# Attention and gated block on one core: the third block's end in halves, projections ahead of a part's rest, units in the last block, rows and weights fetched ahead

## The chip, the core and the metric

The kernel runs on one core of a Trainium2 chip. Its engines work side by side, each on its own list of instructions in order, and wait for one another through semaphores: TensorE (PE) multiplies matrices, VectorE (DVE) and ScalarE (ACT) work element by element, GpSimd (POOL) takes a few element-wise steps, SyncE (SP) issues transfers. The metric is the device time of one execution in microseconds; lower is better.

## The reference

The input x has 2048 rows of 640 bf16 values. A is attention with 32 heads of 20 columns, B a gated product of two projections of width 1728.

```python
h  = x + A(layernorm(x), wqkv, wo)
h2 = h + B(layernorm(h), w_gate, w_up, w_down)
# A: q, k, v = x @ wqkv; p = softmax(q @ k.T * 20 ** -0.5); o = p @ v; o @ wo
# B: g = x @ w_gate; u = x @ w_up; (g * u) @ w_down
```

## The kernel before

The 2048 queries are four blocks of 512 (`NB`, `QB`). The heads are eight groups of four (`NG`, `HPG`), each head in a slot of 32 partitions, so that four heads' score matmuls run in four row strips of the array. A segment is one group's scores of one block against all keys. `PASS` says which query columns a segment's name stands for: "0" to "3" are whole blocks, "A" and "B" the two halves of the last block. The order of `segs` is the order of the attention work: blocks 0, 1 and 2 over all groups, then block 3 whole for two groups (`SPLIT_G`), then its half A for the other six, then its half B. The score columns are cut into 683 tiles of 1536 (three PSUM banks), two tiles in flight. The main loop runs over the tiles: `emit_S` issues the score matmuls (L490) and the exponential of the tile on ACT (L503), `emit_AV` the products with the values (L677) of a tile two or three back, and `run_job` fits other PE work between them, in pieces.

A tile can give its last bank of 512 columns to DVE: `emit_x` computes these exponentials in four DVE operations (L528, L537, L538, L533). Such a piece is called a unit here. `x_takes` (L514) decides by the planner's times (`at`) whether DVE is free; in the last block it takes a unit only where no job is queued or running.

The planner works out the whole order in Python while the program is built: `at` holds its estimate of when PE, DVE and ACT are done, `jobs` is the queue of PE work, `urgent` goes ahead of it, `waiting` holds jobs that stand aside until their input should be ready, `aux` holds DVE work done in spare time, `later` runs a step some tiles on. `keep_warm` (L460) issues two matmuls that nobody reads where PE would idle (recorded at L463).

A finished segment is normalised. Most go through `norm`: the sums of the exponentials travel to DRAM and back (SP: sums, r16, scr, four of bc), DVE takes reciprocals, and POOL multiplies into `On` (L600). The last one of a part (`FAST`) is done by `job_norm` on PE (L608, L624, L639). A block's multiply waits until the projection of the block before has read `On` (the key "om").

When a part is normalised, `add_tail` queues its rest: rows of x and weights are loaded ("load"), `job_out` projects with wo and adds x (L914, L918), takes the layer norm in `aux` and transposes (L271), `job_glu` makes gate times up (`glu_sum`, groups of 512 columns, L980; `glu_pair`, both products of 256 columns in one bank, L998), `job_y` multiplies with w_down (L1035, L1039) and stores. All of these share one PSUM bank, `mi`. The parts are blocks 0, 1 and 2 and the last block's first half (row tiles 0 and 1). Its second half is done after the last exponential by `last_tail`; while its layer norm runs on DVE and ACT, `fill` lets PE finish the jobs that are left over. At the first tile of the last block `load_res` fetches the weights of the column groups 3 to 6 into the buffers of q, which are free by then.

Of the kernel before, what the change touches and what calls it, by code (L numbers as in the profile page):

```python
# [56 lines left out]
EXP_NS, EXP_END, EXP_COL = 50, 166, 5 / 6  # L57
S_NS, S_EXP, SWITCH, LAT = 323, 500, 110, 150
TOL, LEAST, MARGIN = 200, 430, 100
WO_NS, SUMS_NS, ROOT_NS, ROWS_NS = 1500, 6000, 5000, 5000  # L60
END_OF_TIME = 10 ** 9
X_LEAST, X_OUT, X_SOON = 3, 6, 4
# [15 lines left out]
def kernel(  # L78
# [233 lines left out]

    PASS = {"0": (0, 0, QB), "1": (1, 0, QB), "2": (2, 0, QB), "3": (3, 0, QB), "A": (3, 0, HW), "B": (3, HW, HW)}
    segs = []
    for ch in range(NB):
        for g in range(G1):
            kind = "copy" if ch == 0 else "last" if ch == NB - 1 else "add"
            segs.append(("0", g, ch * TPB, (ch + 1) * TPB, kind))  # L320
    segs += [("0", g, 0, NT, "only") for g in range(G1, NG)]
    segs += [(p, g, 0, NT, "only") for p in "12" for g in range(NG)]
    segs += [("3", g, 0, NT, "only") for g in range(SPLIT_G)]
    segs += [(p, g, 0, NT, "only") for p in "AB" for g in range(SPLIT_G, NG)]
    FINAL = len(segs) - 1
    FAST = {("2", NG - 1), ("A", NG - 1), ("B", NG - 2)}

    tiles, cur_t, pos = [], [], 0
    for s, (p, g, lo, hi, _) in enumerate(segs):
# [56 lines left out]
    def step():  # L386
        if cur["fresh"] and (first() or waiting):
            if cur["gen"] is not None:
                jobs.appendleft((cur["key"], cur["gen"]))
            cur["key"], cur["gen"] = (urgent if first() else waiting).popleft()  # L390
        c = advance()
        if c == WAIT:
            waiting.append((cur["key"], cur["gen"]))
            cur["gen"] = None
            c = advance() if jobs and jobs[0][0][0] == "y" else NEXT
        if c is None:
            return None
# [67 lines left out]
    def run_job(until):  # L465
        if cur["fresh"]:
            key = urgent[0][0] if first() else cur["key"] if cur["gen"] is not None else jobs[0][0] if jobs else None
            begin = max(at["pe"], at["mi"], opens.get(key, 0))
            if not waiting and key not in free_keys and (key is None or begin + SWITCH + COST.get(key[0], LEAST) > until):
                return key is not None  # L470
        begun = at["pe"]
        while at["pe"] + 216 <= until + 60:
            c = step()
            if c == FREE and cur["key"][0] not in ("spill", "load"):
                return run_job(until)
            if c in (None, NEXT, END, FREE):
                break
        return at["pe"] > begun

    def emit_S(i):  # L480
# [29 lines left out]
        for s, kt, j, o in us:  # L510
            if o < n_act:
                av_q.append((i, s, kt, j, e[:, o:o + PASS[segs[s][0]][2]]))

    def x_takes(i):  # L514
        us, n = tiles[i]
        s = us[-1][0]
        return (n == EW and segs[s][4] == "only" and (PASS[segs[s][0]][0] < LAST_B or not jobs and not cur["gen"]) and last_tile[s] - i >= X_LEAST and len({u[0] for u in us}) == 1
                and len(x_open) < 2 and at["dve"] < at["pe"] + TOL and len(x_live) < X_OUT)

    def emit_x(ps, us):  # L520
# [46 lines left out]
    def need_x(s):  # L567
        while x_left.get(s):
            step_x()

    def norm(s, asb):
        p, g = segs[s][0:2]
        b, c0, w = PASS[p]
# [9 lines left out]
        def back():  # L583
            if at["pe"] < due and now["i"] < n_tiles:
                later(1, back)
                return
            ri = nrm.tile([P, n], F32, name="ri", tag=f"ri{n}")
            dve(240)
            nc.vector.reciprocal(ri[:], r16)
            scr = dram.tile([HPG, w], F32, name="scr", tag=f"scr{w}")  # L590
            nc.sync.dma_start(scr[:].rearrange("j (c f) -> (j c) f", f=n), ri[:])
            bc = nrm.tile([P, QB], F32, name="bc")
            for j in range(HPG):
                nc.sync.dma_start(bc[SLOT * j:SLOT * (j + 1), 0:w], scr[j:j + 1, :].to_broadcast([SLOT, w]))

            def mult():
                if b and ("om", b - 1) not in done:
                    later(1, mult)
                    return
                nc.gpsimd.tensor_tensor(On[g][:, c0:c0 + w], asb[:, 0:w], bc[:, 0:w], ALU.mult)  # L600
                done.add(("n", p, g))
            later(8, mult)
# [24 lines left out]
    def job_norm(s, asb):  # L627
# [7 lines left out]
        ps = rows_to_cols(bc, w, bank())  # L635
        yield 1030 * w // QB
        dve(690 * w // QB)
        assert b == 0 or ("om", b - 1) in done
# [239 lines left out]
    def open_late():  # L878
        rx.release()
        ra.release()  # L880
        late["wd"] = pool("lwd", side="right")
        late["w"] = pool("lw", 2, side="right")
        late["h"] = pool("lh", side="right")
        late["s"] = pool("ls", 2, side="right")
        late["Wd"] = [late["wd"].tile([P, D], BF16, name=f"wd{f}") for f in range(2 * FP)]

    def load_wd():
# [2 lines left out]
            nc.sync.dma_start(late["Wd"][f][0:rows, :], B_w_down[f * P:f * P + rows, :])  # L890

    def new_st(rows_of):
        hp = late["h"]
        st = {"rows": rows_of, "xr": {}}
        st["ln2T"] = hp.tile([P, KT, QB], BF16, name="ln2T")
# [40 lines left out]
    def job_out(on, st, ts, key):  # L936
# [32 lines left out]

    def load_res():  # L970
        for k, fp in enumerate(range(RES0, FP)):
            late["res"][fp] = [w_tile(src, fp, qkp.tile([P, QA], BF16, name=f"qa{2 * k + m}", tag=f"qa{2 * k + m}"))
                               for m, src in enumerate((B_w_up, B_w_gate))]

    def glu_sum(st, fp, f2, k, c0, n, hold):
        w = min(FPW, FF - fp * FPW)
# [29 lines left out]
                yield 216 * n // QB  # L1006
        yield NEXT

    def job_glu(st, ts, order=tuple(range(FP))):
        c0, n = ts[0] * P, len(ts) * P  # L1010
        hold = {}
        if "hh" not in st:
# [39 lines left out]

    LAST_B, LAST_T = NB - 1, [2, 3]

    def add_tail(b, ts):
        if b == 0:
            do(("open",), open_late)
        key = (b, ts[0])

        def ready():  # L1060
            if b not in tail_st:
                tail_st[b] = new_st(rows_of(b))
                tail_st[b]["res"] = late["res"]
            load_tail(tail_st[b], ts)
            load_w(0, tail_st[b])
            if b == 0:
                load_w(1, tail_st[b])
                load_wd()

        def lazy(fn):  # L1070
            yield from fn(tail_st[b])
        early = b == LAST_B and ("y", b - 1, 0) in done and ("y", b - 1, 1) not in done
        if early:
            free_keys.add(("load",) + key)
            urgent.append((("load",) + key, once(ready)))
        else:
            do(("load",) + key, ready)
        if b == 0:
            add(("pause",), slots(3))
        out = ("out",) + key, lazy(lambda st: job_out(On, st, ts, key))  # L1080
        if early:
            urgent.append(out)
        else:
            jobs.append(out)
        add(("glu",) + key, lazy(lambda st: job_glu(st, ts)))
        if b == LAST_B:
            do(("loadB",), load_last)
        if b == LAST_B:
            y = lazy(lambda st: job_y(st, ts))
            add(("y",) + key, some(y, 2 * len(ts) - 1))  # L1090
            held.append((("y", b, "end"), y))
        else:
            for k in range(2):
                add(("y", b, k), lazy(lambda st, k=k: job_y(st, ts[2 * k:2 * k + 2])))
        if b == 0:
            for g in range(NG):
                do(("spill", g), lambda g=g: spill(g))
# [106 lines left out]
    b_seen, a_seen = 0, False  # L1204
    i = 0
    while i < n_tiles or av_q:
        now["i"] = i
# [17 lines left out]
        if b_seen < NB - 1 and normed(str(b_seen), range(NG)):  # L1225
            add_tail(b_seen, list(range(TPB)))
            b_seen += 1
        if not a_seen and normed("3", range(SPLIT_G)) and normed("A", range(SPLIT_G, NG)):
            add_tail(LAST_B, [0, 1])
            a_seen = True  # L1230
# [111 lines left out]
```

## Time and profile before

| | us |
|---|---|
| median of 3 runs | 939.32 (938.56 to 939.32) |
| the profiled execution, its own time | 938.44 |
| its span, first to last instruction | 936.4 |
| first exponential starts | 15.66 |
| last exponential ends | 894.12 |
| from there to the end of the span | 42.3 |
| ACT busy | 887.8 |
| PE busy | 818.6 |
| DVE busy | 620.7 |

The page gives busy times of the engines and, in 40 slices of the span, their busy shares in tenths. A line of a group names the source line, the engine, the operation, what it writes and reads, the shapes and the count; behind the first bar stand busy time and mean duration in ns, behind the second the idle time just before and who ended it. PE busy is not PE at its peak, since matmuls overlap.

### The profile page before, as it was taken

Reading aid. Unit: us, or ns where it says so; the run is one execution under the profiler, and the core shown is the slowest. Engines: PE = TensorE matmul, PEld = TensorE weight load, DVE = VectorE, ACT = ScalarE, POOL = GpSimd, SP = SyncE. Lnnn points to the kernel's source line nnn. Section 1 sums busy time; section 2 is a strip of 40 time slices with the busy share of each in tenths; the row PEclk is TensorE's granted clock in tenths of the full one; section 3 lists DMA queues with packets and bytes.
Section 4 is the critical chain, followed back from the end, with each engine's and each line's share of the span. In section 5 each row is a group of like instructions: output and inputs, shape, how many; then the busy total and the mean of one; then the engine's idle time right before and its main releaser. Section 6 shows DMA issues by size and latency. Waiting matters only on the chain.

```text
span 936.4 us, 18059 instructions
## 1 busy us (share of the span) xinstructions
PE 818.6 (87%) x7138; PEld 321.7 (34%) x7219; DVE 620.7 (66%) x1222; ACT 887.8 (95%) x719; POOL 61.6 (7%) x155
## 2 busy tenths in 40 slices
PE   8788888888987898998898898998888889978897
PEld 5233232222232222332233222332332334435565
DVE  7674359898888888887888888887562331133342
ACT  6999999999999999999999999999999999999941
POOL 3310011000000000000000000000000000000000
PEclk9999999999999999999999999999899999999999
DMA  6000010011150022014120312002402000212310
GB/s 190 29 2 1 1 27 25 13 35 27 41 164 7 27 77 63 13 34 169 56 57 2 91 48 62 20 29 62 120 2 70 15 12 20 64 28 56 78 43 18
DMA packets 67818, 44.44 MB, mean 47 GB/s; under 512 B 18504, under 2 KB 63404, under 8 KB 67728
## 3 DMA queue, kind: packets, MB, share of 16 engines
q1 hardware_dynamic: 67728, 43.23, 16.6%
q8 instruction: 58, 0.95, 0.4%
q14 instruction: 32, 0.26, 0.1%
HBM read 35.91 MB, written 7.30 MB: 46 GB/s over the span
## 4 chain that ended last, share of the span: by engine, by line
ACT 51%; PE 24%; issue 18%; DVE 7%; ACTq 0%
ACT E L503 51%; PE sc L490 5%; PE acc L677 4%; PE mi L980 3%; PE mi L1035 3%; PE mi L291 2%; PE f L980 2%; PE f L1035 1%; PE mi L305 1%; PE mi L463 1%; DVE xt L538 1%; DVE st L193 1%; DVE u L258 1%; DVE kT L298 1%; PE mi L998 1%
## 5 line engine op out<-in xcount | busy, mean ns | idle before, releaser
L503 ACT ACTIVATE E<-sc 128x1536 bf16<-128x1536 f32 (+1 forms) x683 | 870.3, 1459 | 8.8 <-PE sc L490 6.4
L490 PE MATMUL sc<-qa,kT 32*128 32x512 bf16 x1536 | 201.1, 384 | 47.5 <-ACT E L503 37.0
L490 PEld LDWEIGHTS <-kT 32*128 32x128 bf16 x2432 | 83.8, 91 | 282.8 <-issue 236.1
L677 PE MATMUL acc<-E,vx 128*32 128x512 bf16 (+1 forms) x2305 | 168.2, 351 | 0.5 <-ACT E L503 0.5
L528 DVE TENSOR_SCALAR xv<-sc 128x512 f32<-128x512 f32 x127 | 86.9, 688 | 32.3 <-PE sc L490 31.6
L538 DVE SCALAR_TENSOR_TENSOR xt<-xt,xv 128x512 f32<-128x512 f32 x127 | 92.6, 737 | 0.7
L533 DVE SCALAR_TENSOR_TENSOR xe<-xt,xv 128x512 int16<-128x512 f32 x127 | 90.8, 720 | 0.8
L291 PE MATMUL mi<-lnT,wp 128*128 128x512 bf16 x280 | 81.8, 381 | 10.4 <-DVE kT L298 3.8
L537 DVE SCALAR_TENSOR_TENSOR xt<-xv 128x512 f32<-128x512 uint16 x127 | 87.5, 704 | 0.3
L490 PE MATMUL sc<-qb,kT 32*128 32x256 bf16 (+1 forms) x896 | 69.1, 291 | 16.5 <-ACT E L503 13.3
L600 POOL TENSOR_TENSOR on<-asb,bc 128x512 bf16<-128x512 f32 (+1 forms) x30 | 36.5, 1216 | 694.6 <-DMA bc<-scr 547.7
L677 PEld LDWEIGHTS <-vx 128*32 128x32 bf16 x2432 | 44.4, 95 | 64.3 <-issue 63.8
L1035 PE MATMUL mi<-wd,hh 128*128 128x320 bf16 x364 | 64.3, 302 | 2.0 <-DVE xr L1039 2.0
L258 DVE CAST u<-mi 128x512 bf16<-128x512 f32 (+1 forms) x42 | 29.0, 690 | 36.1 <-PE mi L980 31.7
L1035 PEld LDWEIGHTS <-hh 128*128 128x128 bf16 x448 | 38.4, 97 | 39.9 <-issue 28.3
L980 PE MATMUL mi<-ln2T,wg 128*128 128x512 bf16 (+1 forms) x161 | 45.8, 382 | 6.9 <-DVE u L258 6.4
L463 PE MATMUL mi<-kT,ident 128*128 128x512 bf16 x151 | 48.6, 390 | 1.8 <-issue 0.5
L980 PE MATMUL mi<-ln2T,wu 128*128 128x512 bf16 (+1 forms) x157 | 45.2, 387 | 5.7 <-DVE hh L988 4.7
L988 DVE TENSOR_TENSOR hh<-mi,u 128x512 bf16<-128x512 f32 (+1 forms) x42 | 28.8, 685 | 25.4 <-PE mi L980 22.9
L291 PEld LDWEIGHTS <-wp 128*128 128x128 bf16 x310 | 25.0, 97 | 52.9 <-issue 39.1
L914 PE MATMUL mi<-wo,on 128*128 128x320 bf16 x224 | 38.6, 301 | 2.4 <-DVE xr L918 2.3
L298 DVE TENSOR_SCALAR kT<-mi,one_row 128x512 bf16<-128x512 f32 x30 | 22.4, 746 | 26.7 <-PE mi L291 26.5
(151 smaller groups left out, 582.6 us busy)
## 6 DMA issues: line engine op xcount, KB each, us to landing
bc<-scr SPq DMA_DIRECT2D x100, 64.0 KB
wu<-in_B_w_up_dram SPq DMA_DIRECT2D x20, 320.0 KB
wg<-in_B_w_gate_dram SPq DMA_DIRECT2D x20, 320.0 KB
qsp<-qa SPq DMA_DIRECT2D x8, 384.0 KB
xr<-in_A_x_dram SPq DMA_DIRECT2D x16, 160.0 KB
out_dram<-xr SPq DMA_DIRECT2D x14, 160.0 KB
wd<-in_B_w_down_dram SPq DMA_DIRECT2D x13, 160.0 KB
xs<-in_A_x_dram SPq DMA_DIRECT2D x3, 640.0 KB
```

Of the source, the lines that this page charges most:

```text
L291: nc.tensor.matmul(ps[:], lhsT=wslice(m, g, c), rhs=lnT[:, c, ch * QB:(ch + 1) * QB], start=(c == 0), stop=(c == KT - 1))
L463: nc.tensor.matmul(ps[:], lhsT=ident[:], rhs=kT[0][:, 0:BANK], start=True, stop=True)
L490: nc.tensor.matmul(sc[:, o:o + w], lhsT=kT[g][SLOT * j:SLOT * (j + 1), kt * P:(kt + 1) * P], rhs=q_of(g, b, c0, w)[SLOT * j:SLOT * (j + 1) ...
L503: exps = nc.scalar.activation(e[:, 0:n_act], sc[:, 0:n_act], ACT.Exp, bias=EXP_BIAS, scale=SM_SCALE)
L528: took = nc.vector.tensor_scalar(v[:], ps, X_SCALE, X_BASE, ALU.mult, ALU.max)
L533: nc.vector.scalar_tensor_tensor(e[:], t[:], X_R, v[:], ALU.mult, ALU.add)
L537: lambda: nc.vector.scalar_tensor_tensor(t[:], u, X_P, u, ALU.add, ALU.mult),
L538: lambda: nc.vector.scalar_tensor_tensor(t[:], t[:], X_Q, u, ALU.add, ALU.mult),
L677: nc.tensor.matmul(acc["t"][SLOT * j:SLOT * (j + 1), 0:w], lhsT=vx[kt][:, VS * h:VS * h + SLOT], rhs=e, start=(acc["n"][j] == 0), stop=(ac ...
L914: nc.tensor.matmul(ps[:, 0:HALF], lhsT=on[g][:, t * P:(t + 1) * P], rhs=wo[g][:, cs], start=(g == 0), stop=(g == NG - 1))
L980: nc.tensor.matmul(ps[0:M, 0:n], lhsT=st["w", fp][k][:, c, f2 * P:f2 * P + M], rhs=st["ln2T"][:, c, c0:c0 + n], start=(c == 0), stop=(c == ...
L1035: nc.tensor.matmul(ps[:, 0:HALF], lhsT=st["hh"][f][0:K, t * P:(t + 1) * P], rhs=late["Wd"][f][0:K, cs], start=(f == 0), stop=(f == 2 * FP ...
```

## The change

The third block is now split as the last one was: two groups whole, then two halves "C" and "D" for the other six. Its rest is queued in two parts of two row tiles. A part's projection goes on the urgent queue if its rows are there already (`rows_early` loads them when the part whose buffers they take is queued to its last product), so that it runs ahead of what is left of the part before. A job that stands aside now lets any other part's job go on, where before only the "y" jobs could. Units may be taken in the whole groups and the first half of the last block, and in its second half while a job stands aside. The first weights of the next part are fetched at the last column group of the part before, and the resident weights of the last block one every three tiles instead of all at once. `ln2T` is one buffer for all parts instead of one a part.

```diff
+RES_STEPS = 3
...
-    PASS = {"0": (0, 0, QB), ... "A": (3, 0, HW), "B": (3, HW, HW)}
+    PASS = {"0": (0, 0, QB), ... "C": (2, 0, HW), "D": (2, HW, HW), "A": (3, 0, HW), "B": (3, HW, HW)}
...
-    segs += [(p, g, 0, NT, "only") for p in "12" for g in range(NG)]
-    segs += [("3", g, 0, NT, "only") for g in range(SPLIT_G)]
-    segs += [(p, g, 0, NT, "only") for p in "AB" for g in range(SPLIT_G, NG)]
+    segs += [("1", g, 0, NT, "only") for g in range(NG)]
+    for full, halves in ("2", "CD"), ("3", "AB"):
+        segs += [(full, g, 0, NT, "only") for g in range(SPLIT_G)]
+        segs += [(p, g, 0, NT, "only") for p in halves for g in range(SPLIT_G, NG)]
-    FAST = {("2", NG - 1), ("A", NG - 1), ("B", NG - 2)}
+    TAILS = {0: [0], 1: [0], 2: [0, 2]}
+    FAST = {("C", NG - 1), ("D", NG - 1), ("A", NG - 1), ("B", NG - 2)}
...
-            c = advance() if jobs and jobs[0][0][0] == "y" else NEXT
+            c = advance() if jobs and not any(w[0][1:] == jobs[0][0][1:] for w in waiting) else NEXT
...
-            if not waiting and key not in free_keys and (key is None or begin + SWITCH + COST.get(key[0], LEAST) > until):
+            if waiting:
+                if begin + SWITCH + COST["T"] > until:
+                    return True
+            elif key not in free_keys and (key is None or begin + SWITCH + COST.get(key[0], LEAST) > until):
                 return key is not None
...
+    def X_LAST(p):
+        return p != "B" or bool(waiting)
...
-  ... (PASS[segs[s][0]][0] < LAST_B or not jobs and not cur["gen"]) ...
+  ... (PASS[segs[s][0]][0] < LAST_B or X_LAST(segs[s][0])) ...
...
+    def read_out(b):
+        return all(("om", b, t) in done for t in TAILS[b])
...
-                if b and ("om", b - 1) not in done:
+                if b and not read_out(b - 1):
...
+        late["ln2T"] = late["h"].tile([P, KT, QB], BF16, name="ln2T")
...
-            x_t = late["s"].tile([P, D], BF16, name="xr", bufs=TPB)
+            x_t = late["s"].tile([P, D], BF16, name="xr", bufs=TPB + 2)
...
-                done.add(("om", key[0]))
+                done.add(("om",) + key)
...
     def load_w(fp, st):
-        if fp in st["res"]:
+        if fp == 0 and "next" in late:
+            st["w", fp] = late.pop("next")
+        elif fp in st["res"]:
...
     def load_res():
         for k, fp in enumerate(range(RES0, FP)):
...
+                later(RES_STEPS * (2 * k + m), one)
...
+            if more and k == FP - 1:
+                ahead = {"res": {}}
+                load_w(0, ahead)
+                late["next"] = ahead["w", 0]
...
+    rows_in = set()
+    HELD_BY = {(1, 0): [(0, 0)], (2, 0): [(0, 2)], (2, 2): [(1, 0)], (3, 0): [(1, 2)]}
...
+    def rows_early(b, ts):
+        key = b, ts[0]
+        if key in HELD_BY and key not in rows_in and all(("y",) + k in done for k in HELD_BY[key]):
+            rows(b, ts)
...
-        early = b == LAST_B and ("y", b - 1, 0) in done and ("y", b - 1, 1) not in done
...
-        if early:
+        if key in rows_in:
             urgent.append(out)
         else:
+            if b == 0:
+                do(("open",), open_late)
+            do(("load",) + key, ready)
...
+    due = [("0", range(NG), 0, [0, 1, 2, 3]), ("1", range(NG), 1, [0, 1, 2, 3]), ("C", range(SPLIT_G, NG), 2, [0, 1]),
+           ("D", range(SPLIT_G, NG), 2, [2, 3]), ("A", range(SPLIT_G, NG), 3, [0, 1])]
...
+        if due:
+            rows_early(*due[0][2:])
+        while due and normed(*due[0][0:2]) and (len(due[0][1]) == NG or normed(str(due[0][2]), range(SPLIT_G))):
+            add_tail(*due.pop(0)[2:])
```

More of the change, by code (lines that the diff above doesn't have):

```diff
@@ L311, in job_V @@
         yield 136 * KT
-    PASS = {"0": (0, 0, QB), "1": (1, 0, QB), "2": (2, 0, QB), "3": (3, 0, QB), "A": (3, 0, HW), "B": (3, HW, HW)}
+    PASS = {"0": (0, 0, QB), "1": (1, 0, QB), "2": (2, 0, QB), "3": (3, 0, QB),
+            "C": (2, 0, HW), "D": (2, HW, HW), "A": (3, 0, HW), "B": (3, HW, HW)}
     segs = []
@@ L516, in x_takes @@
         s = us[-1][0]
-        return (n == EW and segs[s][4] == "only" and (PASS[segs[s][0]][0] < LAST_B or not jobs and not cur["gen"]) and last_tile[s] - i >= X_LEAST and len({u[0] for u in us}) == 1
+        return (n == EW and segs[s][4] == "only" and (PASS[segs[s][0]][0] < LAST_B or X_LAST(segs[s][0])) and last_tile[s] - i >= X_LEAST and len({u[0] for u in us}) == 1
                 and len(x_open) < 2 and at["dve"] < at["pe"] + TOL and len(x_live) < X_OUT)
@@ L637, in job_norm @@
         dve(690 * w // QB)
-        assert b == 0 or ("om", b - 1) in done
+        assert b == 0 or read_out(b - 1)
         nc.vector.tensor_tensor(On[g][:, c0:c0 + w], asb[:, 0:w], ps[:, 0:w], ALU.mult)
@@ L892, in new_st @@
     def new_st(rows_of):
-        hp = late["h"]
-        st = {"rows": rows_of, "xr": {}}
-        st["ln2T"] = hp.tile([P, KT, QB], BF16, name="ln2T")
+        st = {"rows": rows_of, "xr": {}, "ln2T": late["ln2T"]}
         return st
@@ L971, in load_res, with one @@
         for k, fp in enumerate(range(RES0, FP)):
-            late["res"][fp] = [w_tile(src, fp, qkp.tile([P, QA], BF16, name=f"qa{2 * k + m}", tag=f"qa{2 * k + m}"))
-                               for m, src in enumerate((B_w_up, B_w_gate))]
+            two = []
+            for m, src in enumerate((B_w_up, B_w_gate)):
+                def one(k=k, fp=fp, m=m, src=src, two=two):
+                    two.append(w_tile(src, fp, qkp.tile([P, QA], BF16, name=f"qa{2 * k + m}", tag=f"qa{2 * k + m}")))
+                    if m:
+                        late["res"][fp] = two
+                later(RES_STEPS * (2 * k + m), one)
     def glu_sum(st, fp, f2, k, c0, n, hold):
@@ L1007, in glu_pair, with job_glu @@
         yield NEXT
-    def job_glu(st, ts, order=tuple(range(FP))):
+    def job_glu(st, ts, order=tuple(range(FP)), more=False):
         c0, n = ts[0] * P, len(ts) * P
@@ L1053, with rows @@
     LAST_B, LAST_T = NB - 1, [2, 3]
+    rows_in = set()
+    HELD_BY = {(1, 0): [(0, 0)], (2, 0): [(0, 2)], (2, 2): [(1, 0)], (3, 0): [(1, 2)]}
+    def rows(b, ts):
+        if b not in tail_st:
+            tail_st[b] = new_st(rows_of(b))
+            tail_st[b]["res"] = late["res"]
+        load_tail(tail_st[b], ts)
+        rows_in.add((b, ts[0]))
+    def rows_early(b, ts):
+        key = b, ts[0]
+        if key in HELD_BY and key not in rows_in and all(("y",) + k in done for k in HELD_BY[key]):
+            rows(b, ts)
     def add_tail(b, ts):
-        if b == 0:
-            do(("open",), open_late)
         key = (b, ts[0])
         def ready():
[L1061 to L1065, printed above, removed]
+            if key not in rows_in:
+                rows(b, ts)
             if b == 0:
+                load_w(0, tail_st[b])
                 load_w(1, tail_st[b])
@@ L1071, in lazy @@
             yield from fn(tail_st[b])
-        early = b == LAST_B and ("y", b - 1, 0) in done and ("y", b - 1, 1) not in done
-        if early:
[L1074 to L1079, printed above, removed]
         out = ("out",) + key, lazy(lambda st: job_out(On, st, ts, key))
-        if early:
+        if key in rows_in:
             urgent.append(out)
         else:
+            if b == 0:
+                do(("open",), open_late)
+            do(("load",) + key, ready)
+            if b == 0:
+                add(("pause",), slots(3))
             jobs.append(out)
-        add(("glu",) + key, lazy(lambda st: job_glu(st, ts)))
+        add(("glu",) + key, lazy(lambda st: job_glu(st, ts, more=b < LAST_B)))
         if b == LAST_B:
             do(("loadB",), load_last)
-        if b == LAST_B:
             y = lazy(lambda st: job_y(st, ts))
@@ L1092, in add_tail @@
         else:
-            for k in range(2):
-                add(("y", b, k), lazy(lambda st, k=k: job_y(st, ts[2 * k:2 * k + 2])))
+            for t in ts[::2]:
+                add(("y", b, t), lazy(lambda st, t=t: job_y(st, [t, t + 1])))
         if b == 0:
@@ L1203 @@
     first_last = next(k for k, (us, _) in enumerate(tiles) if PASS[segs[us[0][0]][0]][0] == LAST_B)
-    b_seen, a_seen = 0, False
+    due = [("0", range(NG), 0, [0, 1, 2, 3]), ("1", range(NG), 1, [0, 1, 2, 3]), ("C", range(SPLIT_G, NG), 2, [0, 1]),
+           ("D", range(SPLIT_G, NG), 2, [2, 3]), ("A", range(SPLIT_G, NG), 3, [0, 1])]
     i = 0
@@ L1224 @@
         run_events(i)
[L1225 to L1230, printed above, removed]
+        if due:
+            rows_early(*due[0][2:])
+        while due and normed(*due[0][0:2]) and (len(due[0][1]) == NG or normed(str(due[0][2]), range(SPLIT_G))):
+            add_tail(*due.pop(0)[2:])
         if i < n_tiles:
```

## The prediction

> **What bounds the kernel now.** I read the page first, then ScalarE's groups by shape, then a table by stage, then the timeline at the end of the run.
>
> ```profile
> span 936.4 us, 18059 instructions
> ...
> PE 818.6 (87%) x7138; PEld 321.7 (34%) x7219; DVE 620.7 (66%) x1222; ACT 887.8 (95%) x719; POOL 61.6 (7%) x155
> ...
> DVE  7674359898888888887888888887562331133342
> ACT  6999999999999999999999999999999999999941
> POOL 3310011000000000000000000000000000000000
> PEclk9999999999999999999999999999899999999999
> ```
> ACT is full from the first slice to the 38th. DVE is full until slice 28 and then drops to 1 to 3 tenths, which is the last block. So the run is a row of exponentials plus what lies before and behind it.
>
> ```profile
> L503 ACT ACTIVATE E<-sc 128x1536 bf16<-128x1536 f32 x555 | 769.9, 1536 | 6.6 <-PE sc L490 4.8 <-ACT E L503 0.3
> L503 ACT ACTIVATE E<-sc 128x1024 bf16<-128x1024 f32 x128 | 138.2, 1123 | 2.2 <-PE sc L490 1.5
> ```
> The second group is the tiles that gave 512 columns, a "unit", to DVE (127 of them; the 128th is the last, short tile). One unit shortens an exponential from 1536 to 1123 ns, 0.413 us, and costs DVE four operations of some 0.7 us. Waits are only 8.8 us in total. Taking units away from ACT is therefore worth nearly its full price, wherever PE and DVE can follow.
>
> Next, the busy time by stage: second block, third block to its seventh part, the rest of the third block, the last block's whole groups, its first half, its second half, and the end.
>
> ```profile
> 239.20:451.70 212.50, 187.15 (x1428) 61.46 (x1445) 178.54 (x320) 210.10 (x172) 11.87 (x8) 0.99 0.23 69
> 451.70:502.90 51.20, 44.85 (x365) 15.97 (x368) 45.95 (x99) 51.20 (x43) 2.85 (x2) 1.00 0.16 38
> 502.90:661.20 158.30, 140.34 (x1068) 46.73 (x1081) 134.62 (x225) 156.63 (x129) 8.84 (x6) 1.00 0.21 55
> 661.20:720.70 59.50, 52.03 (x405) 19.57 (x406) 27.33 (x82) 58.14 (x45) 1.27 (x1) 0.94 0.19 52
> 720.70:807.80 87.10, 78.57 (x961) 34.06 (x971) 22.70 (x42) 86.92 (x65) 4.90 (x6) 1.00 0.09 24
> 807.80:894.20 86.40, 73.22 (x1025) 39.94 (x1031) 26.69 (x81) 86.17 (x66) 2.90 (x4) 1.00 0.19 51
> 894.20:936.40 42.20, 35.22 (x285) 26.30 (x284) 16.46 (x49) 9.85 (x24) 0.00 (x0) 0.97 0.12 34
> ```
> The columns are length, then PE, PEld, DVE, ACT and POOL busy, granted clock, DMA share and GB/s. The last block's two halves hold 128 tiles without units in 173.5 us, 1.355 us a tile; the second block holds 171 tiles with 49 units in 212.5 us, 1.243 a tile. The difference over 171 tiles, 19.2 us, makes 0.39 us a unit with all waits that units bring (0.385 worked with the tile starts themselves). That is the lower price; 0.413 is the upper one.
>
> **Units.** Up to about the 395th of 683 tiles the built program's instructions stand in the same order in both kernels, so nothing before 515 us moves. Behind that, counted in the built order between the same tile numbers: in the third block's two halves 40 units become 29, in the last block's whole groups 2 become 11, in its first half 0 become 15, in its second half 0 become 4. Sum: 127 become 144, 17 more. At 0.385 the stages change by +4.2, -3.5, -5.8 and -1.5, in all **-6.5 us**; at 0.413 it is -7.0. I take -6.5, since it holds the waits of a stage as full as these will be. DVE has the room: in the last block's 233 us it is busy for 76.7, and 28 more units add 28 x 4 x 0.71 = 80.
>
> **Third block in halves.** Scores and values: 384 matmuls of 512 columns become 768 of 256. Rows of the last block price it: 768 of 256 took 51.8 us, 1536 of 512 took 201.1, so 0.067 against 0.131, even. The gate and up products of that block go from groups of 512 to pairs of 256: PE 9.7/70 = 0.139 us a matmul against 17.5/63 = 0.28 for 512 columns, even; DVE 2 x 0.425 a pair, 23.8 us against 14 x (0.691 + 0.685) = 19.3, also beside ACT. The normalisation through PE is done twice at half width (0.5 + 0.6 us against 1.06 + 1.13), even. What matters is where the work lands. In 502.9 to 661.2 PE had 140.3 - 13.6 (44 recorded keep-warm matmuls) = 126.7 us of real work, 80%. The first half's projection (32 matmuls at 0.172), its transposes (10 at 0.09) and seven pairs (70 at 0.139) now fall there, 16 us, so about 88%. The stage at 720.7 was at 90% real work and ACT idled for 0.2 us of 87. Bounds: ACT's present idle of 1.7 us there vanishes (-1.3, with 0.2% left), or its idle share becomes that of the stage at 661.2, 2.3% (+3.6). I take **+0.4**, near the row at 720.7.
>
> **Rows and weights ahead.** No row of PE's or DVE's waits names a DMA above 0.6 us, so fetching earlier saves 0. It adds four loads of w_up and four of w_gate, and five more chains of sums, scr and bc on SP (35 issues). Weight loads stand in SP's queue until PE frees their buffer: 29.5 us in 20 waits, the longest 7.2. Behind them stand the chain's DMAs, and behind those POOL's multiply. Its result is needed some 6 to 7 tiles after a half ends, but it is landed by then by about 5 tiles (6.6 us); a 7.2 us wait at the wrong place would cost up to 0.6. Taken at 0. Spreading the eight loads of resident weights over 22 tiles leaves the first pair 10 tiles ahead of its use; 0.
>
> **The end.** The first half's last-block output has three of its four half tiles left when the exponentials stop, against two: 42 matmuls instead of 28 between the projection and the transposes.
>
> ```profile
> 900.18 4.28 PE L1035 MATMUL f<-wd,hh 128*128 128x320 bf16 x28
> 902.48 1.13 DVE L1155 TENSOR_SCALAR ln<-f,m,rstd 128x320 bf16<-128x320 f32 x2
> 902.64 1.12 ACT L1156 ACTIVATE ln<-f,mr,rstd 128x320 bf16<-128x320 f32 x2 [0.48 <-DVE mr L1151]
> 904.40 0.45 PE L271 MATMUL mi<-ident,ln 128*128 128x128 bf16 x5
> 905.91 9.01 PE L980 MATMUL f<-ln2T,qa 128*128 128x256 bf16 x80 [0.78 <-ACT ln2T L255]
> ```
> The cover of these matmuls is the layer norm, which is ready at 903.76, and the 28 already outlast it. So 14 more at 4.28/28 = 0.153 push everything behind by **+2.1 us**. The third half tile needs a bank back; the first one's is read by 904.0, ahead of need. Had the cover been longer it would cost nothing; if the bank came late, 0.5 more.
>
> **Sum.** -6.5 + 0.4 + 2.1 = -4.0. Against the profiled execution's 938.44 that is 934.4. The median of the three runs, 939.32, lies 0.9 above it; on that scale I predict 935.3.
>
> **Rivals.** *A, the gain is larger.* At 667.35 the granted clock fell to half for 6.8 us, just behind the third block's end; the stage at 661.2 took 59.5 us where 43 x 1.353 - 2 x 0.385 = 57.4 was due, so a dip costs about 2.0. In the new order that seam has eight value matmuls and the next projection between its small matmuls, so the dip may go: -7.0 + 2.1 - 2.0 = -6.9, 932.4.
>
> *B, nothing comes of it.* There are now three seams (ends of the third block's first half, of its second, of the last block's first) instead of two where PE runs little but scores and tiny matmuls, and 20 pairs of keep-warm matmuls are gone. Two more dips: -4.0 + 4.0 = 0, 939.3. For it: the dip at 667.35. Against: the seam at 808 to 815 us shows none. The Trainium skill (TensorE: Matmul & The Clock Gate, What's actually happening) says the clock halves after an idle window of about 3.4 us. The trace agrees on the period (half-rate stretches of 3.41 and 6.83 us), but PE was 82% busy by its records in the window before the second one.
>
> *C, slower.* DVE loses time to POOL, and PE stands behind DVE:
>
> ```profile
> 572.62 1.34 POOL L600 TENSOR_TENSOR on<-asb,bc 128x512 bf16<-128x512 f32 x1 [25.79 <-DMA bc<-scr]
> 572.75 1.75 DVE L538 SCALAR_TENSOR_TENSOR xt<-xt,xv 128x512 f32<-128x512 f32 x1
> 575.16 0.81 PE L980 MATMUL mi<-ln2T,wu 128*128 128x512 bf16 x3 [1.31 <-DVE hh L988]
> 576.39 1.02 ACT L503 ACTIVATE E<-sc 128x1024 bf16<-128x1024 f32 x1 [0.77 <-PE sc L490]
> ```
> The multiply made a 0.74 us operation last 1.75, and ACT lost 0.77. The Trainium skill (SBUF — State Buffer, Who interferes with whom) has DVE and GpSimd lock a shared pair of ports, the second one blocked for the whole instruction; this row agrees. In the new kernel 17 multiplies (2 whole, 15 half as wide, 0.73 us against 1.34) meet units behind the 384th tile. If each costs ACT as here by its length, 2 x 0.77 + 15 x 0.42 = 7.8: +3.8, 943.1. It decides from 5.9/17 = 0.35 us each. Against it: the second block has 8 multiplies among 49 units, and ACT idles for 2.4 us in all.
>
> That the units don't come is excluded by the built order.
>
> **Numbers.** About 0.2%, 1.9 us, is what a measurement can tell here. Forecast 0.55, A 0.20, B 0.12, C 0.13. Faster takes the forecast but for a twentieth of it, and A: 0.72; same takes B and the slow edge of the forecast: 0.15; slower is C: 0.13. The range runs from a little below A (931.6) through B to a little above it (940.6); half of C and little else is left out.
>
> **What would show it.** ACT: 145 short and 538 long exponentials; last exponential ending near 888 us; stages as above (the third block's halves 4 us longer, the last block 11 shorter); 42 matmuls and a gap of 44.4 us from the last exponential to the end. Wrong would be: ACT waits for sc well over 10 us, more half-rate windows than two, or PE waiting for POOL's on.

## The result and the profile after

| | before | after |
|---|---|---|
| median of 5 runs each | 939.32 us (938.56 to 939.71) | 943.98 us (942.37 to 945.22) |
| ratio of the times, 95% interval | | 1.0049 (1.0034 to 1.0063) |
| profiled execution, its span | 938.44, 936.4 | 945.22, 943.4 |
| mean granted clock of that execution | 0.993 | 0.984 |

The changed kernel is slower by 0.5%, 4.7 us. The forecast was 4.0 us faster.

The page of the changed kernel, then ScalarE's two shapes of exponential:

```profile
span 943.4 us, 20070 instructions
...
PE 832.4 (88%) x8087; PEld 348.2 (37%) x8087; DVE 668.8 (71%) x1333; ACT 882.6 (94%) x719; POOL 62.2 (7%) x160
...
DVE  7673358898888888888887667777688667372342
...
PEclk9999999999999999999999999899899999998999
```
```profile
L510 ACT ACTIVATE E<-sc 128x1536 bf16<-128x1536 f32 x538 | 747.3, 1525 | 16.7 <-PE sc L497 14.5 <-ACT E L510 0.2
L510 ACT ACTIVATE E<-sc 128x1024 bf16<-128x1024 f32 x145 | 153.8, 1097 | 2.8 <-PE sc L497 1.5 <-ACT E L510 0.3
```
The units came as counted, 145 short and 538 long, and ACT is busy 5.2 us less than before. DVE works on at 6 to 8 tenths through the last block's whole groups and its first half, where it had dropped to 1 to 3 in most slices. But ACT's idle time ahead of the exponentials has risen from 8.8 to 19.5 us, 16 of them waiting for scores, and the clock row shows three weak slices (the 26th, 29th and 37th) where there was one (the 29th).

The stages, by the same tiles as in the prediction (third block's two halves, last block's whole groups, its first half, its second half, the end; columns as there):

```profile
503.10:670.10 167.00, 151.10 (x1891) 66.59 (x1891) 118.36 (x234) 161.93 (x129) 8.67 (x10) 0.97 0.21 56
670.10:726.40 56.30, 50.02 (x429) 21.37 (x429) 47.06 (x103) 53.94 (x45) 2.42 (x2) 0.94 0.27 70
726.40:810.00 83.60, 74.59 (x1007) 38.40 (x1006) 57.54 (x108) 81.20 (x64) 4.63 (x5) 1.00 0.17 43
810.00:899.20 89.20, 75.02 (x1009) 39.11 (x1009) 35.52 (x94) 84.92 (x65) 3.65 (x5) 0.96 0.17 43
899.20:943.40 44.20, 37.38 (x299) 27.65 (x298) 16.94 (x50) 10.06 (x25) 0.00 (x0) 0.97 0.11 32
```
Against before: +8.7 (4.6 forecast with the +0.4), -3.2 (-3.5), -3.5 (-5.8), +2.8 (-1.5), +2.0 (+2.1). The two stages that are worst against the forecast have a granted clock of 0.97 and 0.96, where it was 1.00 before (the whole groups had 0.94 in both kernels). PE's waits name something that the kernel before did not have, the weights (the first line is the kernel before, the others the changed one):

```profile
ACT E L503 <- PE sc L490: 6.4, 13, 0.8
...
ACT E L510 <- PE sc L497: 16.1, 23, 3.2
...
PEld L1017 <- DMA wu<-in_B_w_up_dram: 4.9, 3, 2.5
...
PE mi L1017 <- DMA wu<-in_B_w_up_dram: 2.7, 2, 2.2
```
Columns: who waits for whom, us in total, times, the longest. Before, ACT waited for scores for 6.4 us in all, at most 0.8 at once, and no wait of PE named a weight load. One of the places, from the timeline:

```profile
846.53 0.72 PE L1017 MATMUL mi<-ln2T,wu 128*128 128x256 bf16 x5
...
847.52 0.34 SPq L604 DMA_DIRECT2D scr<-ri  x1
...
848.99 1.71 SPq L607 DMA_DIRECT2D bc<-scr  x4
...
850.74 0.42 SPq L972 DMA_DIRECT2D wu<-in_B_w_up_dram  x1
...
854.74 0.99 PE L1017 MATMUL mi<-ln2T,wu 128*128 128x256 bf16 x5 [2.18 <-DMA wu<-in_B_w_up_dram]
...
856.75 0.62 PE L497 MATMUL sc<-qb,kT 32*128 32x256 bf16 x6
...
857.48 1.45 ACT L510 ACTIVATE E<-sc 128x1536 bf16<-128x1536 f32 x1 [3.15 <-PE sc L497]
```
The part's gate and up products begin at 846.53 with column group 0, which was fetched ahead. The weights of group 1 are issued only when the products have begun. On SP they stand behind a norm's trip to DRAM and back, so they go at 850.74, 4.2 us behind the first product. SP had stood from 841.1 to 847.5 for DVE's reciprocals, which the norm's `scr` takes; when the load's turn came, it waited for nothing of its own. Half-wide products use up a group in about 6 us, and the weights are there at 854.7. PE stands for 2.18 us, the scores behind it are late, and ACT loses 3.15. The score matmuls that follow take 0.62 us for six instead of 0.40: the clock has gone to half for 6.8 us. Before, the same fetch stood ahead of that norm in the queue and was issued at 840.08, 1.9 us *ahead* of the first product at 841.94, and nothing waited at 847.84:

```profile
840.08 0.43 SPq L960 DMA_DIRECT2D wu<-in_B_w_up_dram  x1
...
841.94 0.72 PE L998 MATMUL mi<-ln2T,wu 128*128 128x256 bf16 x5
```
That part was half as wide in the kernel before too, so its width alone does not make a load late.

This happens in all three half-wide parts (at 660, 748 and 855 us). The load left 3.9 us behind the part's first product at the first of them, again behind a norm's `scr` and `bc`, and 2.0 us behind it at the second, where PE's longest wait for weights is 0.5 us and the clock holds. Set beside the shortest interval of each shape of exponential (1.330 and 0.903 us from start to start), the tiles behind the 384th lose 24.1 us in the changed kernel and 11.6 before. The larger part of that lies at six places: the three weight waits with what follows (2.8, 1.3 and 4.4 us) and three places of half clock alone, at 589, 678 and 715 us (2.2, 1.2, 1.6). The balance of the spans is -7.3 (units, by those intervals) + 12.4 + 1.8 (end) + 0.1 (ahead of the 384th tile) = +7.0.

The windows of 3.4 us before a half-rate stretch, at a weight wait, at the third block's seam, and at a pair of transposes:

```profile
851.60:855.00 3.40, 1.22 (x26) 0.71 (x26) 0.85 (x2) 2.73 (x2) 0.72 (x1) 1.00 0.76 191
585.40:588.80 3.40, 2.76 (x45) 1.42 (x40) 3.18 (x8) 3.23 (x4) 1.02 (x1) 1.00 0.06 19
711.70:715.10 3.40, 1.90 (x24) 0.87 (x22) 3.23 (x7) 3.40 (x4) 0.27 (x1) 1.00 0.57 138
```
PE's busy time is the second figure after the length: 1.22, 2.76 and 1.90 us of 3.40. Behind the 384th tile and ahead of the end there are five such half-rate stretches, 24 us in all (6.8 at 589 and at 855, 3.4 at 660, 678 and 715); before there was one of 6.8.

### The profile page after: what moved, and what is told of

The parts are those of the page before. It is cut to its first block, busy times and chain, and to the rows that moved or that the text cites. A ratio compares the mean times of both kernels' runs of the same rounds, so it can differ in the third digit from the quotient of the medians.

```text
span 943.4 us, 20070 instructions
## 1 busy us (share of the span) xinstructions
PE 832.4 (88%) x8087; PEld 348.2 (37%) x8087; DVE 668.8 (71%) x1333; ACT 882.6 (94%) x719; POOL 62.2 (7%) x160
## 4 chain that ended last, share of the span: by engine, by line
ACT 44%; PE 31%; issue 15%; DVE 8%; DMA 1%; SPq 0%; ACTq 0%
ACT E L510 44%; PE sc L497 7%; PE acc L690 5%; PE mi L1058 4%; PE mi L999 3%; PE mi L1017 3%; PE mi L292 2%; PE f L999 2%; PE f L1058 2%; PE mi L306 1%; DMA wg<-in_B_w_gate_dram 1%; DVE xt L548 1%; PE mi L926 1%; DVE st L194 1%; PE mi L467 1%
## 5 line engine op out<-in xcount | busy, mean ns | idle before, releaser
L510 ACT ACTIVATE E<-sc 128x1536 bf16<-128x1536 f32 (+1 forms) x683 | 865.1, 1434 | 19.5 <-PE sc L497 16.1
L497 PE MATMUL sc<-qa,kT 32*128 32x512 bf16 (+1 forms) x1920 | 203.3, 341 | 41.7 <-ACT E L510 32.8
L690 PE MATMUL acc<-E,vx 128*32 128x256 bf16 (+1 forms) x2624 | 172.8, 329 | 0.6 <-ACT E L510 0.6
L538 DVE TENSOR_SCALAR xv<-sc 128x512 f32<-128x512 f32 x144 | 98.8, 688 | 47.1 <-PE sc L497 45.3
L548 DVE SCALAR_TENSOR_TENSOR xt<-xt,xv 128x512 f32<-128x512 f32 x144 | 102.5, 719 | 0.8
L543 DVE SCALAR_TENSOR_TENSOR xe<-xt,xv 128x512 int16<-128x512 f32 x144 | 102.2, 714 | 0.9
L547 DVE SCALAR_TENSOR_TENSOR xt<-xv 128x512 f32<-128x512 uint16 x144 | 101.3, 717 | 0.3
L613 POOL TENSOR_TENSOR on<-asb,bc 128x256 bf16<-128x256 f32 (+1 forms) x35 | 37.1, 1059 | 698.3 <-DMA bc<-scr 433.8
L690 PEld LDWEIGHTS <-vx 128*32 128x32 bf16 x2816 | 56.5, 96 | 67.3 <-issue 66.6
L497 PE MATMUL sc<-qb,kT 32*128 32x256 bf16 (+1 forms) x896 | 69.7, 293 | 11.6 <-ACT E L510 10.8
L1022 DVE CAST u<-mi 128x256 bf16<-128x256 f32 (+1 forms) x42 | 17.7, 422 | 40.3 <-PE mi L1017 39.9
L690 PE MATMUL acc<-xe,vx 128*32 128x512 bf16 (+1 forms) x192 | 44.5, 330 | 0.0
```

The source lines that it names most:

```text
L497: nc.tensor.matmul(sc[:, o:o + w], lhsT=kT[g][SLOT * j:SLOT * (j + 1), kt * P:(kt + 1) * P], rhs=q_of(g, b, c0, w)[SLOT * j:SLOT * (j + 1) ...
L510: exps = nc.scalar.activation(e[:, 0:n_act], sc[:, 0:n_act], ACT.Exp, bias=EXP_BIAS, scale=SM_SCALE)
L538: took = nc.vector.tensor_scalar(v[:], ps, X_SCALE, X_BASE, ALU.mult, ALU.max)
L543: nc.vector.scalar_tensor_tensor(e[:], t[:], X_R, v[:], ALU.mult, ALU.add)
L547: lambda: nc.vector.scalar_tensor_tensor(t[:], u, X_P, u, ALU.add, ALU.mult),
L548: lambda: nc.vector.scalar_tensor_tensor(t[:], t[:], X_Q, u, ALU.add, ALU.mult),
```

## The experiments

Two theories after the result. **W**: the weights of group 1 come late in half-wide parts. **S**: the new seams and light stretches drop the clock. A third, **U**, was that units in the last block do not pay, and rival C of the prediction is a fourth. Experiments 1 to 4 ran on one chip, 5 to 8, 9 to 11 and 12 on others, each beside runs of the kernel before, whose medians there were 939.58, 939.57, 938.40 and 938.40; the ratios are to these. The runs of the result are a group of their own. Differences between groups are less sure than those within one.

**1. The second group ahead as well.** The changed kernel, in which the part before also fetches group 1 of the next part, behind its own last product. Only the order on SP differs: in the traces of the two kernels PE, DVE, ACT and POOL run the same instructions in the same order.

```diff
-        if fp == 0 and "next" in late:
-            st["w", fp] = late.pop("next")
+        if ("next", fp) in late:
+            st["w", fp] = late.pop(("next", fp))
...
+        if more:
+            fetch(1)        # a new tile and its two loads, kept in late["next", 1]
```


> The changed kernel, but at the end of a part's gate and up products the weights of the next part's column group 1 are fetched too, not only those of group 0; PE's, DVE's and ACT's order is untouched. Theory W (the halves use a group of weights in half the time, the fetch of group 1 starts only with the products and comes late three times, and two of these waits drop the clock): exponentials 506 to 510, 570 to 574 and 652 to 655 lose 2.8, 1.3 and 4.4 us less, in all -8.6, so 935.4 us; PE waits for wu and wg under 1 us in all; no half-rate clock at 660 and 855 us. Theory U (28 units are too much for PE and DVE in the last block): nothing changes, 944. Theory S (the clock falls at the seams whatever the weights do): -3 at most, 941.

Measured: 938.57 us, ratio 0.9983 (0.9960 to 1.0006), 5.4 us less than the changed kernel. The time misses the 935.4 that was expected, while the rest came: in PE's waits, loads of the weights are down to a single 0.2 us, the half-rate stretches at 660 and 855 are gone, and ACT's wait for scores falls:

```profile
ACT E L510 <- PE sc L497: 5.2, 14, 0.8
```
W is right, and rival C goes with it: units and POOL's multiplies are what they were in the changed kernel, and the 10.9 us of ACT's waiting went with the weights and, in this execution, the clock. What remains is a spread: ten executions of this one kernel took 932.3 to 940.7 us, in step with the clock. The three at 0.997 averaged 932.5, the three at 0.986 939.5. 1.1% of 936 us is 10.3 us of lost clock, or 20.6 us at half rate, for 7.1 us of time: 0.34 us per us at half rate. At an equal clock (0.985 to 0.989), the changed kernel's four runs average 943.5 and this one's five 939.3, so 4.2 us is what the waits alone cost, and up to 6.8 more lies in the clock.

**2. Holding the clock at the seams.** The changed kernel with two matmuls that nobody reads ahead of the scores of 14 tiles around the three seams (448 to 452, 514 to 518, 544 to 547); the scores overwrite them.

```diff
+        for k in range(2 if i in SEAM else 0):
+            nc.tensor.matmul(sc[:, k * BANK:(k + 1) * BANK], lhsT=ident[:], rhs=kT[0][:, 0:BANK], start=True, stop=True)
```


> The changed kernel with two more 512-column matmuls that nobody reads ahead of the scores of 14 tiles around the ends of the third block's two halves and the transposes behind them (28 x 0.22 = 6 us of PE where it idles). Theory S: the half-rate windows at 589, 678 and 715 us go, exponentials 453 to 455, 519 to 521 and 548 to 550 lose 2.2, 1.2 and 1.6 us less, -5.0, so 939 us, while the dips at 660 and 855 behind the weight waits stay. Theory W alone: below -1. Theory U: slower by up to 3, since PE gets more work.

Measured: 945.58, ratio 1.0056 (1.0039 to 1.0072). The three half-rate stretches at the seams are gone, yet the time is no better. The extra matmuls hold up the scores of full tiles (0.85 us at exponential 449, 0.89 at 514, some 4 us in all), and at the last weight wait ACT loses 4.2 us here, with half-rate stretches of 6.8 and 10.2 us behind the weight waits. The expectation of 939 missed by 6.6 us: the remedy's price had been taken at nearly nothing, and the weight waits cost more than before (exponentials 506 to 510 and 652 to 655 lose 10.1 us against 7.3).

**3. Both.**

> The two edits together: group 1 of the weights ahead and warm matmuls at the seams. If W and S hold and add up: -13.6, so 930.4 us, faster than the kernel before by 0.9%. If U holds: 944 or more.

Measured: 936.30, ratio 0.9964 (0.9950 to 0.9978); its profile shows no half-rate stretch ahead of the end. Weights in time and the clock held do make it faster than before, but 6 us less so than expected; about 4 of these are the matmuls of experiment 2.

**4. Units out of the last block.** The changed kernel with the old rule there (9 units instead of 30; 123 in all).

```diff
     def X_LAST(p):
-        return p != "B" or bool(waiting)
+        return not jobs and not cur["gen"]
```


> The changed kernel with the old rule for units in the last block (only where no job is queued or running): 9 instead of 30 there, 123 in all. W and S: 21 units at 0.385 are missed, +8.1; only one of four half tiles is left for the end instead of three, -2.7; so +5.4, 949 us, with the weight waits still there. U: faster than the changed kernel by 3 us or more, 941 or less.

Measured: 949.15, ratio 1.0077 (1.0050 to 1.0104), 5.2 us above the changed kernel. The expected +5.4 (8.1 for 21 units, less 2.7 at the end) came. In the profiled executions the last exponential ends 7.6 us later, 0.36 a unit, and the end behind it is 3.1 us shorter (41.0 against 44.1). U is refuted.

**5. The same in the kernel of experiment 3.**

> The kernel with both edits (group 1 of the weights ahead, warm matmuls at the seams), but with the old rule for units in the last block: 123 units instead of 144. Compared with both edits alone (936.3). The unit price as predicted, 0.385: 21 x 0.385 = +8.1, and two half tiles fewer at the end, -2.7, so 941.7 us. Theory U (units in the last block cost more than they bring): 936 or less.

Measured: 944.96, ratio 1.0048 (1.0024 to 1.0072), 8.7 us above experiment 3, where 5.4 was expected; U is refuted here too. The profile has three half-rate stretches ahead of the end where experiment 3's has none: 3.4 us at 65 and at 410, where the two kernels are alike, and 6.8 at 891. The first two make the 384th tile 1.8 us later. The last exponential ends 12.1 us later and the end is 3.0 shorter; without those 1.8 and some 2 for the third stretch (an estimate by rival A's price of a dip), 8.3 us are left for 21 units, 0.39 each. So a unit in the last block is worth 0.36 to 0.39 us in the two experiments, near the 0.385 of the prediction.

**6. Units alone, in the kernel before.** There they can go into the last block's whole groups only.

```diff
-... (PASS[segs[s][0]][0] < LAST_B or not jobs and not cur["gen"]) ...
+... (PASS[segs[s][0]][0] < LAST_B or segs[s][0] == "3" or not jobs and not cur["gen"]) ...
```


> The kernel before with units in the last block's two whole groups only (8 more, 135 in all), the third block whole as it was: one part of the change alone. By the predicted prices: -8 x 0.385 = -3.1, one half tile more at the end (42 matmuls), +2.1, so -1.0 and 938.5 us. Theory U: slower than before by 2 or more.

Measured: 939.83, ratio 1.0007 (0.9991 to 1.0024): no difference that could be told. In the profile, the whole groups shrink from 59.5 to 55.1 us, and the second half grows from 86.3 to 89.2, with half-rate stretches at 813 and 837; here too 42 matmuls come between the projection and the transposes at the end. One stage's gain went into the clock and the end. The expected -1.0 and U's +2 lie too close to either side of the result for it to decide between them.

**7 and 8. Fewer extra matmuls.** Both are experiment 1 with extra matmuls: one in each of 11 tiles (450 to 453, 516 to 518, 544 to 547), or two in each of 7 tiles where PE has little else (450 to 452, 518, 545, 547, 548).

> Group 1 of the weights ahead, and one warm matmul instead of two ahead of the scores of 11 tiles, only where PE has little at the three seams. If the two warm matmuls of before delayed the scores (exponentials 447 to 449, 514, 517 and 543 each 0.5 to 0.9 us late, 4 in all) and one is enough to keep the clock: 932.5 us with no half-rate window. If one isn't enough: the windows at 590, 675 or 712 us come back in some executions, 935 to 939, with a wide spread.

> Group 1 of the weights ahead, and two warm matmuls ahead of the scores of only those seven tiles behind which PE had nothing to do. If it is the place that costs and not the matmuls: 932.5 us with no half-rate window. Otherwise 936, as with 28 of them.

Measured: 936.09, ratio 0.9952 (0.9935 to 0.9969), runs from 932.7 at 0.997 to 937.5 at 0.990; and 935.41, ratio 0.9938 (0.9913 to 0.9962), from 932.0 at 0.999 to 936.7 at 0.992. Both medians lie below that of experiment 1, by 2.5 and 3.2 us, on another chip. Neither reached the 932.5 that was named for a clock that holds. Their profiles have half-rate stretches, but elsewhere now: at 409, 508, 809 and 880, and at 409, 808 and 880. A seam that is held does not hold the others.

**9 and 10. The clock held in both kernels.** Experiment 1 with two extra matmuls in 19 tiles, at places where dips had been seen (224, 226 to 228, 311, 313, 314, 450 to 452, 518, 545, 547, 548, 622, 624, 676 to 678); and, as a control, the kernel before with as many in 18 tiles, at the places that leave PE with little to do there.

> Group 1 of the weights ahead, and two warm matmuls ahead of the scores of 19 tiles, all of those where the granted clock fell in any execution so far (around the transposes at the 226th and 313th tile, the three seams, the end). If the rest of the spread is the half-rate clock: about 931.5 us, faster than the kernel before by 0.8%, and the runs lie within 2 us of one another. If the warm matmuls cost what they save: 936.

> The kernel before with the same warm matmuls at 18 tiles where it leaves PE with little to do: the control for the kernel above. If the gain comes from the clock alone, this one reaches the same time, 932. If it comes from units, which are no part of it: 936.5, since the kernel before has two half-rate windows or so at 0.3 us a us.

Measured: 935.92, ratio 0.9977 (0.9965 to 0.9990), and the control 939.79, ratio 1.0013 (1.0000 to 1.0025), both at a clock of 0.994 to 0.999. The first came out at the 936 named for matmuls that cost what they save, and its runs spread over 4.2 us; the control lies above both values named for it. A steadier clock gives the kernel before nothing that outweighs what the matmuls cost it (939.79 against 938.40 without them). The repaired change is 3.9 us ahead of the control in the medians, 3.7 in the spans (932.9 against 936.6), and 2.5 ahead of the kernel before without extra matmuls. The repaired change's stages (third block's halves, whole groups, first half, second half):

```profile
504.20:667.10 162.90, 146.05 (x1878) 66.15 (x1896) 117.79 (x235) 161.50 (x130) 8.66 (x10) 1.00 0.21 53
667.10:721.40 54.30, 48.34 (x433) 21.36 (x437) 46.26 (x103) 53.70 (x45) 1.99 (x2) 1.00 0.32 84
721.40:803.60 82.20, 74.14 (x1005) 38.57 (x1006) 56.18 (x108) 81.08 (x65) 4.18 (x5) 1.00 0.17 44
803.60:889.20 85.60, 72.77 (x1012) 38.73 (x1019) 35.63 (x94) 84.90 (x65) 3.63 (x5) 1.00 0.14 37
```
and of the control those two that differ from the page before:

```profile
662.10:720.20 58.10, 51.28 (x409) 19.84 (x412) 27.16 (x82) 57.64 (x44) 1.27 (x1) 1.00 0.19 53
...
807.30:894.10 86.80, 76.22 (x1034) 40.68 (x1040) 26.74 (x81) 86.17 (x65) 2.90 (x4) 1.00 0.20 51
```
With the clock at 1.00 in all of them, the stages differ by +4.5 (162.9 against the control's 158.4), -3.8, -4.9 and -1.2. The prediction had +4.6, -3.5, -5.8 and -1.5.

**11. The end.** Experiment 9, in which two of the three left-over half tiles run ahead of the transposes and the third behind them.

```diff
-        fill()
+        fill(2)
...   # the transposes of the last part
+        fill()
```


> The kernel with group 1 ahead and 19 warm tiles, and at the end only two half tiles of the first half's output ahead of the transposes, the third behind them. By the prediction's own step for the end, 14 x 0.153 = 2.1 us then stand behind the copies of the transposed tiles, where PE waited 0.8 us anyway: -0.8 against the kernel above.

Measured: 933.84, ratio 0.9947 (0.9933 to 0.9961). From the last exponential's end to the end of the span it is 42.7 us instead of 43.6, 0.9 less as expected; the medians differ by 2.1, and the rest stays unexplained.

**12. The best version.** Experiment 11 with the extra matmuls in 12 tiles only (226 to 228, 450 to 452, 518, 545, 547, 548, 622, 624).

> As the kernel with the third half tile later (933.84), but warm matmuls at 12 tiles only: those at the tiles 311, 313, 314 and 676 to 678, whose scores came 0.4 to 0.6 us late behind them, are left out. If these delays (2.0 us in all) were the warm matmuls' own: 932. If the clock falls there again now and then: up to 935, with a wider spread.

Measured: 932.73, ratio 0.9937 (0.9919 to 0.9954), the lowest median of all, near the 932 expected, and 0.6% under the kernel before; its six runs took 930.8 to 935.7 at clocks of 1.0 to 0.992. The profiled one has one half-rate stretch of 6.8 us, at 825.

Not tried apart: whether group 1 is late through its place behind the norm's DMAs on SP or through being issued so near its use; experiment 1 takes both away. At the third place the traces speak for the queue: the norm held SP for 9.6 us there, from 841.1 to 850.7, while the buffer was free long before (in experiment 1, with PE's order the same, it took this load at 779.9), and a load of 4 us that left by 848 would have been in time for 852.6. For the other two places it stays open.

## Why the prediction was wrong

- **"Rows and weights ahead ... taken at 0" is the step that failed.** Its reason, that no wait of PE or DVE in the kernel before named a DMA above 0.6 us, held for that order only: there group 1's weights were issued 1.9 us ahead of the last block's half-wide part. Only group 0 was moved ahead, and the part's products follow at once. With the step put right, the medians move by 5.4 us (experiment 1), 4.2 at an equal clock. The step did look at SP's queue, but at what stands *behind* weight loads there (the norms' DMAs), not at weight loads that stand behind a norm, and not at when the second group is first needed: about 6 us on, against 4 us from issue to landing. The kernel before had a row for it, more than three times the 29.5 us of weight loads that the prediction quotes (`scr` waiting for the reciprocals):

```profile
SPq L591 <- DVE ri L589: 98.7, 25, 6.7
```
- **The clock had too small a place.** It stood in rivals A and B as one dip more or less, or two more. The changed kernel has five stretches where there was one, 24 us against 6.8, and two of them follow a weight wait. B's price, 2.0 us for 6.8 us at half rate, is 0.29 a us; 0.34 was measured. The 17 us more are then worth 5 to 6 us, of which those behind the weight waits belong to the step above. With 4.2 us for the waits at an equal clock, this makes 9 to 10 us, where forecast and median are 8.7 apart (the stretches are counted in the profiled execution, 1.2 us above that median). Weights in time alone are not the forecast: experiment 1 is 1.0 us under the kernel before on its chip, and its mean clock falls lower (0.984 to 0.997, against 0.988 to 0.996). B's argument against itself, that the seam at 808 to 815 showed no dip, was one execution's: with units alone (experiment 6) the kernel before has a half-rate stretch at 813, in that seam. Experiment 1 shows one kernel anywhere between 932 and 941 us, in step with its mean clock.
- **Rival C gave 943.1, close to the time measured, by a mechanism that costs little here.** In experiment 1 the multiplies meet the same units and ACT's waiting is 5.2 us in all, less than before; no wait of PE for POOL's on stands out.
- **Units: right.** 17 more, as counted, and 0.36 to 0.39 us each by experiments 4 and 5. By the stages of experiments 9 and 10, the units and the third block's halves together gave -5.4 where -6.1 was forecast.
- **Third block in halves: right.** +4.5 with the clock held, 4.6 forecast (4.2 for eleven units fewer and 0.4 for a fuller PE). The upper bound of +3.6 that was given for a fuller PE is ACT's whole idle time at 2.3%; the change from the present 1.7 us would be +1.9. The sum does not use it. The +8.7 of the changed kernel holds the dip at 589 and the weight wait at 660.
- **The end: right.** +2.0 against +2.1, with 42 matmuls (6.39 us) ahead of the transposes; experiment 11 gets 0.9 of it back.

The sum of -4.0 thus describes the change with its weights in time and the clock held in both kernels: -3.9 between experiments 9 and 10. For the change as it was made it left out the largest term. "ACT waits for sc well over 10 us" and "more half-rate windows than two" were named as signs of it, and both came.

## What to carry to other kernels

When a step is made half as wide, the time in which it uses up each prefetched buffer halves with it: a whole part of the kernel before needed its second group 12 us behind its first product (512.4 to 524.4), a half-wide one 6. List for every buffer when it is first needed and when its load can leave the queue, with what the queue waits for ahead of it, and not for the first one alone. A row that shows no wait for a transfer is evidence for the order in which it was taken, not for a new one. Where ACT or another engine is the bound and PE is nearly as full, a stall of PE can be paid twice, once as the wait and once at half clock behind it, as at 660 and 855 us, though not at 748; a difference of half a per cent needs the clock of each run beside its time.

## What was not expected of the hardware

- One kernel without any change spread over 8.4 us (experiment 1, 932.27 to 940.72) with the granted clock between 0.997 and 0.984. The Trainium skill (TensorE: Matmul & The Clock Gate, What's actually happening) says that the window of the gate is free-running, that it does not reset when a kernel starts, and that the ramp at the start costs under 1% of a typical span. The traces agree on the window: in each profiled execution all half-rate stretches start on one grid of 3.413 us (588.81, 660.49, 677.55, 715.10 and 855.05 in the changed kernel are 21, 5, 11 and 41 periods apart), and the grid lies differently against the kernel from one profile to the next. The spread is not the ramp at the start; it is 0.9% of 936 us, twice the effect under study.
- A PE that is 81% busy by its records (2.76 us of 3.40 at 585.4) still lost its clock. That window holds score matmuls on 32 rows and four products of four columns. What such matmuls count for was not measured apart, and it stays open which windows drop.
- Two extra matmuls of 512 columns ahead of a full tile's scores cost ACT up to 0.9 us (experiment 2): a remedy for the clock is not free where ACT waits closely on PE.
